# GpSimd's scaling of the softmax rows: a multiply by one column becomes a multiply by one column and an add of a column of zeros

## The chip, the cores and the metric

One core of a Trainium2 chip runs the whole program. The metric is the time of one execution on the device in microseconds; the time before is 1647.33 us, the median of 2 runs (1647.22 to 1647.44). The engines are called as the profile calls them: PE (TensorE), DVE (VectorE), ACT (ScalarE), POOL (GpSimd) and SP (SyncE, which only issues DMAs here).

## The reference

Attention over 8 batches of 8 heads, 576 positions and head size 64, with a threshold below each row's maximum, and then a feed-forward net over the 4608 tokens of 512 numbers:

```python
scores = scale * np.matmul(q, k.transpose(0, 1, 3, 2))
thresh = np.max(scores, axis=-1, keepdims=True) - tau
scores = np.where(scores >= thresh, scores, -1000000000.0)
scores = scores - np.max(scores, axis=-1, keepdims=True)
attn = np.exp(scores)
attn = attn / (np.sum(attn, axis=-1, keepdims=True) + 1e-09)
attn_out = np.matmul(attn, v)                  # 8, 8, 576, 64
x = attn_out.transpose(0, 2, 1, 3).reshape(4608, 512)
h = x @ w_in                                   # 512 to 2048
r = np.maximum(h, 0.0)
out = (s * (r * r) + b) @ w_out                # 2048 to 512
```

All is fp32.

## The kernel before, in words

The work of attention is cut into 288 tiles of 128 query rows by 576 keys. The first 36 (batch 0, "plain") use fp32 matmuls as they are. The other 252 split each operand into a high part, rounded to fp32r, and a low part, the rest, and multiply the parts; this needs more element-wise work and less of PE.

One tile i goes through the engines so. PE makes the scores into PSUM (L324). DVE copies them negated to SBUF and takes the row's minimum into a column of st (L327). ACT makes the threshold column (L331) and the exponential em (L333). DVE zeroes what lies beyond the threshold, multiplies with em and sums the rows (L336), and takes the reciprocal of the sums (L339). POOL then multiplies em, 128 x 576, in place by that column of reciprocals (L340): this is the instruction that is changed, one for each tile, 288 in all. For a split tile DVE then transposes em in blocks of 32 x 32 (L371 for 512 columns, L373 for 64), SP's queue moves the blocks with four DMAs to er (L377), ACT rounds er to eh (L387), and POOL subtracts to get the low part (L388). PE multiplies both with v (L402). For a plain tile PE transposes em (L348, L349). The tiles sm, em and tr have two buffers each, so tile i + 2 takes the buffers of tile i; the scores lie in one bank pair after the first 16 tiles.

The feed-forward net runs between: 18 blocks of 256 tokens, 16 steps each. A step is 12 matmuls (L518), Relu (L525), Square (L527) and rounding (L528) on ACT, a low part on POOL (L529 gl; for the last block on DVE) and 12 matmuls (L535). POOL has one more job, the low part of v (L276). DVE also makes the low parts of k (L272), q and qt (L292) and x (L504), and adds and takes out results (L409, L546).

The order in which each engine gets its instructions is worked out before the program is built. `Plan` is a list scheduler: each operation is added with an engine, a pair of costs in ns (how long it holds its engine, after how long its result is there), its keys read and written, and a due time in tiles; `Plan.run` lets each engine take, of what is ready by these costs, the operation due first. POOL's operations, and those marked `port`, also exclude one another in the plan. Each engine then runs its list strictly in that order, and waits on semaphores where data is not there. So a change of a cost in the plan moves instructions in the lists and changes nothing else.

Of the kernel before, what the change touches and what calls it, by code (L numbers as in the profile page):

```python
# [12 lines left out]
AF = mybir.ActivationFunctionType  # L13
ALU = mybir.AluOpType
# [88 lines left out]
def tile_attention_ffn(ctx: ExitStack, tc: tile.TileContext, qT, kT, v, tau, w_in, w_out, s, b, out):  # L103
    nc = tc.nc
    P = 128
# [22 lines left out]
    def const(name, shape, dt=F32):  # L128
        return cp.tile(shape, dt, name=name)
# [3 lines left out]
    tau_t = const("tau_t", [P, 1])  # L133
    tau0 = const("tau0", [P, 1])
    nsc = const("nsc", [P, 1])
    bias_t = const("bias_t", [P, DM])
    ones = const("ones", [P, P], F32R)
    qt = const("qt", [P, 2, P], F32R)
# [46 lines left out]
    def dve2(cost, fn, r, w, at):  # L185
        plan.add("DVE", cost, fn, r, w, at)

    def act(cost, fn, r, w, at):
        plan.add("ACT", cost, fn, r, w, at)
# [47 lines left out]
    class Head:  # L237
# [30 lines left out]
        def prepare(self, at):  # L268
            j = self.j
            khi, klo = self.kk  # L270
            act((673, 760), lambda: nc.scalar.copy(out=lazy["k"][:, 2 * j], in_=raw), self.rk, [khi], at)
            dve2((760, 830), lambda: nc.vector.tensor_tensor(  # L272
                out=lazy["k"][:, 2 * j + 1], in0=raw, in1=lazy["k"][:, 2 * j].bitcast(F32), op=ALU.subtract),
                self.rk + [khi], [klo], at)
            act((460, 540), lambda: nc.scalar.copy(out=vt[:, j, :, 0], in_=rv), self.rv, self.kv, at)
            pool((922, 950), lambda: nc.gpsimd.tensor_tensor(  # L276
                out=vt[:, j, :, 1], in0=rv, in1=vt[:, j, :, 0].bitcast(F32), op=ALU.subtract), self.rv + self.kv, self.kv, at)
            self.load_q(at)
            self.q = {}
            parts = []  # L280
            for u in self.halves:
                n = count["q"] % 2
                count["q"] += 1
                self.q[u] = (n, [f"q{n}"])
                parts.append((slice(u * NB, (u + 1) * NB), qs[n], f"q{n}", (400, 480), (500, 560)))
            if self.tail:
                self.qt = [f"qt{j}"]
                parts.insert(min(1, j), (slice(M, S), qt[:, j, j * T:(j + 1) * T], f"qt{j}", (244, 320), (300, 360)))
            for cs, dst, key, ca, cd in parts:
                act(ca, lambda dst=dst, cs=cs: nc.scalar.activation(out=dst, in_=raw[:, cs], func=AF.Copy, scale=nsc),  # L290
                    self.rq + ["nsc"], [key], at)
                dve2(cd, lambda dst=dst, cs=cs: nc.vector.scalar_tensor_tensor(  # L292
                    out=dst[D:P], in0=raw[D:P, cs], scalar=nsc[D:P], in1=dst[D:P].bitcast(F32), op0=ALU.mult,
                    op1=ALU.subtract), self.rq + [key, "nsc"], [key], at)
# [15 lines left out]
    def tile_of(ti, i):  # L310
# [8 lines left out]
        def scores():  # L319
# [8 lines left out]
            out=sb_[:, 0:S].rearrange("p (a b) -> p a b", a=2), in0=ps[:, :, 0:HS],  # L328
            scalar1=nsc if plain else 1.0, scalar2=None, op0=ALU.mult, op1=ALU.min, accum_out=st8[:, 0:1]),
            [bk, "nsc"], [sm_k, (ks_, 0)], i - SCORES_AHEAD)  # L330
        act((200, 280), lambda: nc.scalar.activation(out=st8[:, 1:2], in_=st8[:, 0:1], func=AF.Identity, bias=tau0),  # L331
            [(ks_, 0), "nsc"], [(ks_, 1)], i - 0.4)
        act((780, 870), lambda: nc.scalar.activation(  # L333
            out=ev, in_=sb_[:, 0:S], func=AF.Exp, bias=st8[:, 0:1], scale=-1.0),
            [sm_k, (ks_, 0)], [em_k], i - 0.5)
        dve2((970, 1040), lambda: nc.vector.scalar_tensor_tensor(  # L336
            out=eb, in0=sb_, scalar=st8[:, 1:2], in1=eb, op0=ALU.is_le, op1=ALU.mult,
            accum_out=st8[:, 2:3]), [sm_k, em_k, (ks_, 1)], [em_k, (ks_, 2)], i)
        dve((160, 210), lambda: nc.vector.reciprocal(out=st8[:, 4:5], in_=st8[:, 2:3]), [(ks_, 2)], [(ks_, 4)], i)  # L339
        pool((870, 900), lambda: nc.gpsimd.tensor_scalar(  # L340
            out=ev, in0=ev, scalar1=st8[:, 4:5], scalar2=None, op0=ALU.mult), [em_k, (ks_, 4)], [em_k], i)

        if plain:
            tp, tt = bank["tp"].rearrange("p (t q) -> p t q", t=NQ), bank["tt"][0:T, 0:P]
# [25 lines left out]
        def blocks():  # L370
            nc.vector.transpose(out=to[:, :, 0:NQ].rearrange("p m c q -> p m (c q)"),  # L371
                                in_=ev[:, 0:M].rearrange("p (m r) -> p m r", m=4))
            nc.vector.transpose(out=to[:, 0:2, NQ], in_=ev[:, M:S].rearrange("p (m q) -> p m q", m=2))  # L373
        dve((740, 810), blocks, [em_k], [tr_k], i + 0.5)
        t = ti.slot
        for n in range(4):
            plan.add("SP", (450, 2600), lambda n=n: nc.sync.dma_start(  # L377
# [112 lines left out]
    class Block:  # L490
# [4 lines left out]
        def stage(self, at):  # L495
            first = not count["stage"]
            count["stage"] += 1
            more = [("xh", 1), ("xl", 0), ("xl", 1)] + [(x, "t", u) for x in ("xh", "xl") for u in range(2)] if first else []
            for c in range(0, NC, 2):
                sl = slice(c, c + 2)  # L500
                kh, kl = ("xh", c // 2), ("xl", c // 2)
                act((617, 700), lambda sl=sl: nc.scalar.copy(out=xhl()[0][:, sl], in_=self.src[:, sl]),  # L502
                    self.ksrc, [kh] + (more if not c else []), at)
                dve2((710, 780), lambda sl=sl: nc.vector.tensor_tensor(  # L504
                    out=xhl()[1][:, sl], in0=self.src[:, sl], in1=xhl()[0][:, sl].bitcast(F32), op=ALU.subtract),
                    self.ksrc + [kh], [kl], at)

# [166 lines left out]
    def constants():  # L674
        make_identity(nc, ident)
        for t in qd:
            nc.gpsimd.memset(t, 0.0)
        for t in tr + [rv]:
            nc.gpsimd.memset(t, 0.0)
        for t in sm:  # L680
            nc.gpsimd.memset(t[:, S:S + 1], -3e38)
        for t in em:
            nc.gpsimd.memset(t[:, S:S + 1], 1e-9)
# [97 lines left out]
```

## Time and profile before

| | |
|---|---|
| median of the runs | 1647.33 us (1647.22 to 1647.44) |
| the profiled execution, its own time | 1645.36 us |
| its span in the profile | 1643.5 us |
| TensorE's mean granted clock | 0.943 |
| PE busy | 1376.1 us, 84% |
| POOL busy | 1240.6 us, 75% |
| DVE busy | 1119.3 us, 68% |
| ACT busy | 1016.8 us, 62% |

Busy times are sums over the span. They say how much an engine did, not whether anything waited for it: that is read from the waits and from the stretches of the span. A busy PE is not PE at its peak, because matmuls overlap and their ends are modelled. What the profile shows as POOL's spans is rough, so the start of the next instruction is the better mark of an end.

### The profile page before, as it was taken

The page shows a single profiled execution, that of the slowest core. Times are in us where ns is not written, and L with a number is a line of the kernel's source. Part 1 is how long each engine was busy: PE and PEld are TensorE (multiplying, and loading weights), DVE is VectorE, ACT ScalarE, POOL GpSimd, SP SyncE. Part 2 cuts the span into 40 slices and gives each one's busy share as a digit, 9 for nine tenths or more (in the row PEclk, how much of TensorE's full clock was granted, in tenths as well). Part 3 has the DMA queues.
Part 4 walks back from the last instruction along what each step waited for, and adds up shares of the span by engine and source line. Part 5 has one row for each costly group of instructions (what it writes and reads, how often), then busy time and mean ns, then how long its engine had stood idle before and what let it go on. Part 6 is the DMA issues. An engine that isn't in the chain of part 4 may idle for free. (4 is left out here: it accounts for less than half of the span.)

```text
span 1643.5 us, 27906 instructions
## 1 busy us (share of the span) xinstructions
PE 1376.1 (84%) x8221; PEld 1183.7 (72%) x8221; DVE 1119.3 (68%) x2533; ACT 1016.8 (62%) x2371; POOL 1240.6 (75%) x893
## 2 busy tenths in 40 slices
PE   8999878568888888778988687887888789868998
PEld 6677667457776777667876576676777688767897
DVE  6876588777878777776247777777778757756101
ACT  6777566556666667666456666666666657656543
POOL 4554499889889889988369979888988978877410
PEclk9999999669999999999999899998999989999999
DMA  9410244443444434443134434434344433443100
GB/s 317 164 35 1 60 119 107 117 103 94 111 108 106 104 95 120 103 110 78 35 76 108 109 98 98 111 95 111 98 99 108 101 95 97 115 106 98 37 14 14
DMA packets 227016, 159.04 MB, mean 97 GB/s; under 512 B 64560, under 2 KB 204848, under 8 KB 226864
## 3 DMA queue, kind: packets, MB, share of 16 engines
q1 hardware_dynamic: 226864, 157.26, 36.7%
q8 instruction: 66, 1.08, 0.3%
q14 instruction: 86, 0.70, 0.1%
HBM read 65.14 MB, written 9.44 MB: 45 GB/s over the span
## 5 line engine op out<-in xcount | busy, mean ns | idle before, releaser
L340 POOL TENSOR_SCALAR em<-em,st 128x576 f32<-128x576 f32 x288 | 557.8, 1938 | 164.4 <-DVE st L339 118.8
L388 POOL TENSOR_TENSOR er<-er,eh 128x640 fp32r<-128x640 f32 x252 | 409.5, 1627 | 55.8 <-ACT eh L387 53.4
L535 PE MATMUL o<-w,gh 128*128 128x512 f32 x1152 | 372.1, 405 | 11.3 <-DVE oo L546 9.7
L336 DVE SCALAR_TENSOR_TENSOR em<-sm,st,em 128x577 f32<-128x577 f32 x288 | 327.5, 1139 | 38.7 <-ACT em L333 18.2
L371 DVE STREAM_TRANSPOSE tr<-em 128x512 f32<-128x512 f32 x252 | 179.2, 711 | 217.2 <-POOL em L340 202.8
L529 POOL TENSOR_TENSOR gl<-g,gh 128x256 fp32r<-128x256 f32 x272 | 229.1, 848 | 112.6 <-ACT gh L528 49.1
L333 ACT ACTIVATE em<-sm,st 128x576 f32<-128x576 f32 x288 | 223.1, 775 | 141.2 <-DVE sm L327 60.4
L535 PE MATMUL o<-w,gl 128*128 128x512 f32 x576 | 239.0, 415 | 49.6 <-POOL gl L529 49.1
L518 PE MATMUL h<-xh,w 128*128 128x256 f32 x1280 | 270.8, 292 | 9.8 <-ACT g L525 5.2
L387 ACT CAST eh<-er 128x640 fp32r<-128x640 f32 x252 | 182.3, 724 | 141.4 <-DMA er<-tr 136.5
L324 PE MATMUL s<-k,q 128*128 128x288 f32 x896 | 174.1, 319 | 82.4 <-DVE sm L327 73.3
L535 PEld LDWEIGHTS o<-w,gh 128*128 128x128 f32 x1152 | 207.4, 195 | 40.5 <-DVE oo L546 10.6
L518 PEld LDWEIGHTS h<-xh,w 128*128 128x128 f32 x1280 | 219.5, 198 | 16.9 <-ACT g L525 7.5
L324 PEld LDWEIGHTS s<-k,q 128*128 128x128 f32 x896 | 142.7, 201 | 111.9 <-DVE sm L327 87.6
L327 DVE TENSOR_SCALAR_CACHE_REDUCE sm<-s 128x576 f32<-128x576 f32 x252 | 187.8, 745 | 46.9 <-PE s L324 44.9
L518 PE MATMUL tp<-xh,w 128*128 128x256 f32 x1024 | 208.7, 286 | 0.7 <-ACT g L525 0.6
L518 PE MATMUL h<-xl,w 128*128 128x256 f32 x640 | 187.9, 294 | 18.5 <-DVE xl L504 18.4
L535 PEld LDWEIGHTS o<-w,gl 128*128 128x128 f32 x576 | 111.2, 193 | 104.5 <-POOL gl L529 81.5
L518 PEld LDWEIGHTS tp<-xh,w 128*128 128x128 f32 x1024 | 171.3, 194 | 3.2 <-ACT g L525 1.1
L518 PE MATMUL tp<-xl,w 128*128 128x256 f32 x512 | 146.1, 285 | 0.0
L518 PEld LDWEIGHTS h<-xl,w 128*128 128x128 f32 x640 | 126.6, 198 | 24.2 <-DVE xl L504 22.0
L528 ACT CAST gh<-g 128x256 fp32r<-128x256 f32 x288 | 115.2, 401 | 18.3 <-PE o L535 14.1
(144 smaller groups left out, 2237.0 us busy)
## 6 DMA issues: line engine op xcount, KB each, us to landing
er<-tr SPq DMA_DIRECT2D x1008, 80.0 KB, 2.3
raw<-in_k_dram SPq DMA_DIRECT2D x128, 144.0 KB, 2.8
raw<-in_q_dram SPq DMA_DIRECT2D x96, 144.0 KB, 2.8
w<-in_moe_w_in_dram SPq DMA_DIRECT2D x16, 512.0 KB, 8.5
w<-in_moe_w_out_dram SPq DMA_DIRECT2D x16, 512.0 KB, 8.5
rv<-in_v_dram SPq DMA_DIRECT2D x64, 128.0 KB, 2.4
out_dram<-oo SPq DMA_DIRECT2D x32, 256.0 KB, 2.2
rv<-in_v_dram SPq DMA_DIRECT2D x128, 8.0 KB, 2.1
```

The lines of the kernel that those rows point to most:

```text
L324: nc.tensor.matmul(ps[:, hf, 0:HS], stat, kk[:, cs], start=(n == 0), stop=(n == len(seq) - 1))
L327: dve((840, 900), lambda: nc.vector.tensor_scalar(out=sb_[:, 0:S].rearrange("p (a b) -> p a b", a=2), in0=ps[:, :, 0:HS], scalar1=nsc if p ...
L333: act((780, 870), lambda: nc.scalar.activation(out=ev, in_=sb_[:, 0:S], func=AF.Exp, bias=st8[:, 0:1], scale=-1.0), [sm_k, (ks_, 0)], [em_ ...
L336: dve2((970, 1040), lambda: nc.vector.scalar_tensor_tensor(out=eb, in0=sb_, scalar=st8[:, 1:2], in1=eb, op0=ALU.is_le, op1=ALU.mult, accum ...
L340: pool((870, 900), lambda: nc.gpsimd.tensor_scalar(out=ev, in0=ev, scalar1=st8[:, 4:5], scalar2=None, op0=ALU.mult), [em_k, (ks_, 4)], [em ...
L371: nc.vector.transpose(out=to[:, :, 0:NQ].rearrange("p m c q -> p m (c q)"), in_=ev[:, 0:M].rearrange("p (m r) -> p m r", m=4))
L387: act((730, 820), lambda: nc.scalar.copy(out=hi(), in_=lo().bitcast(F32)), ker, [("eh", t)], i + 1)
L388: pool((1640, 1670), lambda: nc.gpsimd.tensor_tensor(out=lo(), in0=lo().bitcast(F32), in1=hi().bitcast(F32), op=ALU.subtract), [("eh", t)] ...
L518: nc.tensor.matmul(ps, w[:, c, :], x[:, c, :], start=(c == 0 and i == 0), stop=(c == NC - 1 and i == 2))
L528: act((400, 480), lambda: nc.scalar.copy(out=hi, in_=g), [f"g{k}"], [f"gh{k}"], at)
L529: do((800, 830), lambda: eng.tensor_tensor(out=lo, in0=g, in1=hi.bitcast(F32), op=ALU.subtract), [f"g{k}", f"gh{k}"], [f"gl{k}"], at)
L535: nc.tensor.matmul(bank["o"][:, t, :], a[:, ts_], w, start=(f == 0 and i == 0), stop=(f == NF - 1 and i == 2))
```

## The change

A constant tile `zero`, 128 x 1, is made and set to zero by POOL at the start. L340 gets a second operation: after the multiplication by the column of reciprocals the column `zero` is added. The values stay what they were. No DMA, no buffer of em and no other engine's operation is added or removed.

Eight pairs of costs in the plan are changed with it: those of DVE's low parts of k (760 to 950), q (500 to 680), qt (300 to 500) and x (710 to 850), of L336 (970 to 1080) and of the transposes (740 to 915), and those of ACT's threshold column (200 to 287) and of its scaling of q and qt (400 to 490, 244 to 320). The plan's cost of L340 stays at 870. The line numbers of the changed kernel are one higher from here on.

```diff
+    zero = const("zero", [P, 1])
...
-            dve2((760, 830), lambda: nc.vector.tensor_tensor(
+            dve2((950, 1020), lambda: nc.vector.tensor_tensor(
                 out=lazy["k"][:, 2 * j + 1], in0=raw, in1=lazy["k"][:, 2 * j].bitcast(F32), op=ALU.subtract),
...
-        dve2((970, 1040), lambda: nc.vector.scalar_tensor_tensor(
+        dve2((1080, 1150), lambda: nc.vector.scalar_tensor_tensor(
...
         pool((870, 900), lambda: nc.gpsimd.tensor_scalar(
-            out=ev, in0=ev, scalar1=st8[:, 4:5], scalar2=None, op0=ALU.mult), [em_k, (ks_, 4)], [em_k], i)
+            out=ev, in0=ev, scalar1=st8[:, 4:5], scalar2=zero, op0=ALU.mult, op1=ALU.add), [em_k, (ks_, 4)], [em_k], i)
...
-        dve((740, 810), blocks, [em_k], [tr_k], i + 0.5)
+        dve((915, 980), blocks, [em_k], [tr_k], i + 0.5)
...
-        for t in tr + [rv]:
+        for t in tr + [rv, zero]:
             nc.gpsimd.memset(t, 0.0)
```

The lists of all engines are longer or shorter by nothing but the one memset, and the feed-forward steps stand among the tiles much as before, but neighbours are exchanged in many places. Two of them, for the tile whose scores were the 123rd:

DVE before, in batch 2; the tile's own rows are those with em_82 and st_74, sm, em, st and tr being the tiles named above and _n the buffer:

```order
L336 SCALAR_TENSOR_TENSOR em_82,st_74<-sm_78,st_74,em_82 128x577
L292 SCALAR_TENSOR_TENSOR qt<-raw,nsc,qt 64x64
L339 RECIPROCAL st_74<-st_74 128x1
L327 TENSOR_SCALAR sm_78,st_76<-s 128x576
L336 SCALAR_TENSOR_TENSOR em_83,st_75<-sm_79,st_75,em_83 128x577
L371 STREAM_TRANSPOSE tr_80<-em_82 128x4x128
L373 STREAM_TRANSPOSE tr_80<-em_82 128x2x32
```

DVE now, the same tile; its rows are those with em_83 and st_75, since every buffer's number is one higher:

```order
L337 SCALAR_TENSOR_TENSOR em_83,st_75<-sm_79,st_75,em_83 128x577
L372 STREAM_TRANSPOSE tr_82<-em_84 128x4x128
L374 STREAM_TRANSPOSE tr_82<-em_84 128x2x32
L340 RECIPROCAL st_75<-st_75 128x1
L328 TENSOR_SCALAR sm_79,st_77<-s 128x576
L293 SCALAR_TENSOR_TENSOR qt<-raw,nsc,qt 64x64
L372 STREAM_TRANSPOSE tr_81<-em_83 128x4x128
L374 STREAM_TRANSPOSE tr_81<-em_83 128x2x32
```

Between the tile's reciprocal, which POOL's multiplication waits for, and the transposes, which wait for the multiplication, stood the next tile's L336; now the low part of qt stands there, and the transposes of the tile before have moved in front of the reciprocal.

POOL before, around the same tile's multiplication (em_82, st_74):

```order
L340 TENSOR_SCALAR em_83<-em_83,st_73 128x576
L529 TENSOR_TENSOR gl_99<-g_95,gh_97 128x256
L529 TENSOR_TENSOR gl_98<-g_94,gh_96 128x256
L388 TENSOR_TENSOR er<-er,eh 128x640
L340 TENSOR_SCALAR em_82<-em_82,st_74 128x576
L529 TENSOR_TENSOR gl_99<-g_95,gh_97 128x256
L388 TENSOR_TENSOR er<-er,eh 128x640
L340 TENSOR_SCALAR em_83<-em_83,st_75 128x576
```

POOL now (em_83, st_75):

```order
L341 TENSOR_SCALAR em_84<-em_84,st_74,zero 128x576
L530 TENSOR_TENSOR gl_99<-g_95,gh_97 128x256
L530 TENSOR_TENSOR gl_100<-g_96,gh_98 128x256
L341 TENSOR_SCALAR em_83<-em_83,st_75,zero 128x576
L389 TENSOR_TENSOR er<-er,eh 128x640
L341 TENSOR_SCALAR em_84<-em_84,st_76,zero 128x576
```

The L388 that stood between the two low parts of feed-forward steps and the tile's multiplication is gone from there, and of the two rows between this multiplication and the next one only the L389 is left.

More of the change, by code (lines that the diff above doesn't have):

```diff
@@ L284, in prepare @@
                 self.q[u] = (n, [f"q{n}"])
-                parts.append((slice(u * NB, (u + 1) * NB), qs[n], f"q{n}", (400, 480), (500, 560)))
+                parts.append((slice(u * NB, (u + 1) * NB), qs[n], f"q{n}", (490, 570), (680, 740)))
             if self.tail:
                 self.qt = [f"qt{j}"]
-                parts.insert(min(1, j), (slice(M, S), qt[:, j, j * T:(j + 1) * T], f"qt{j}", (244, 320), (300, 360)))
+                parts.insert(min(1, j), (slice(M, S), qt[:, j, j * T:(j + 1) * T], f"qt{j}", (320, 400), (500, 560)))
             for cs, dst, key, ca, cd in parts:
@@ L330, in tile_of @@
             [bk, "nsc"], [sm_k, (ks_, 0)], i - SCORES_AHEAD)
-        act((200, 280), lambda: nc.scalar.activation(out=st8[:, 1:2], in_=st8[:, 0:1], func=AF.Identity, bias=tau0),
+        act((287, 370), lambda: nc.scalar.activation(out=st8[:, 1:2], in_=st8[:, 0:1], func=AF.Identity, bias=tau0),
             [(ks_, 0), "nsc"], [(ks_, 1)], i - 0.4)
@@ L503, in stage @@
                     self.ksrc, [kh] + (more if not c else []), at)
-                dve2((710, 780), lambda sl=sl: nc.vector.tensor_tensor(
+                dve2((850, 920), lambda sl=sl: nc.vector.tensor_tensor(
                     out=xhl()[1][:, sl], in0=self.src[:, sl], in1=xhl()[0][:, sl].bitcast(F32), op=ALU.subtract),
```

## The prediction

> **What bounds the kernel now.** The page first: busy shares, and the 40 slices for the engine that the change touches.
>
> ```profile
> PE 1376.1 (84%) x8221; PEld 1183.7 (72%) x8221; DVE 1119.3 (68%) x2533; ACT 1016.8 (62%) x2371; POOL 1240.6 (75%) x893
> ...
> POOL 4554499889889889988369979888988978877410
> ```
>
> POOL's 75% is an average over a quiet start, a long middle at 9 tenths, dips, and an end without it. So I cut the span into four kinds of stretch: the plain batch (0 to 200 us), the middle where POOL is full (200 to 700 and 900 to 1300), the stretches rich in feed-forward work (700 to 900 and 1300 to 1530), and the end. Busy us of each engine, instructions in brackets:
>
> ```profile
> 0.00:200.00 200.00, 187.49 (x1126) 141.48 (x1126) 141.24 (x322) 135.70 (x326) 96.92 (x76) 0.99 0.35 116
> ...
> sum 900.00, PE 722.03 PEld 628.80 DVE 697.82 ACT 574.88 POOL 799.91; mean PE 361.02 PEld 314.40 DVE 348.91 ACT 287.44 POOL 399.96
> ...
> sum 430.00, PE 361.24 PEld 319.06 DVE 264.88 ACT 259.34 POOL 324.99; mean PE 180.62 PEld 159.53 DVE 132.44 ACT 129.67 POOL 162.50
> ...
> 1530.00:1643.00 113.00, 105.31 (x662) 94.36 (x661) 15.32 (x30) 46.92 (x116) 18.80 (x24) 0.98 0.07 19
> ```
>
> In the first stretch PE is busy for 93.7%. In the 900 us of the middle POOL is at 88.9%, PE at 80.2%, DVE at 77.5%: POOL sets the pace. In the 430 us of the third kind PE leads with 84.0%, POOL 75.6%. In the end PE works alone.
>
> Then the waits, to see whether anybody waits for POOL. First over the whole span, then DVE's for 200 to 700 and for 900 to 1300, then PE's for 700 to 900 and for 1300 to 1530 (us in total, times, longest):
>
> ```profile
> DVE tr L371 <- POOL em L340: 202.8, 199, 3.0
> POOL em L340 <- DVE st L339: 118.8, 90, 6.9
> PE s L324 <- DVE sm L327: 77.3, 60, 4.0
> PE tp L348 <- POOL em L340: 2.4, 2, 1.3
> ...
> DVE tr L371 <- POOL em L340: 68.4, 73, 2.0
> ...
> DVE tr L371 <- POOL em L340: 64.8, 66, 2.3
> ...
> PE s L324 <- DVE sm L327: 9.6, 9, 3.7
> PE o L535 <- POOL gl L529: 6.6, 7, 2.5
> PE pv L402 <- POOL er L388: 3.2, 3, 1.4
> PE tt L402 <- POOL er L388: 2.9, 3, 1.4
> ...
> PE o L535 <- POOL gl L529: 7.4, 6, 2.3
> PE tt L402 <- POOL er L388: 5.0, 6, 1.5
> PE s L324 <- DVE sm L327: 2.0, 3, 1.1
> ```
>
> DVE stands 202.8 us in front of its transposes for this very multiplication, 199 times of 252. Behind the waiting transposes on DVE's list is the L327 that empties the score banks, and PE waits 77.3 us for that. So a late L340 reaches PE by way of DVE.
>
> **What one multiplication costs now.** POOL's groups, then the fastest and median L340 (ns), and one place of the timeline that shows the duration against the next start:
>
> ```profile
> L340 POOL TENSOR_SCALAR em<-em,st 128x576 f32<-128x576 f32 x288 | 557.8, 1938 | 164.4 <-DVE st L339 118.8 <-ACT xt L366 7.9 <-PE tt L349 6.1
> L388 POOL TENSOR_TENSOR er<-er,eh 128x640 fp32r<-128x640 f32 x252 | 409.5, 1627 | 55.8 <-ACT eh L387 53.4 <-PE tp L518 1.0 <-DMA raw<-in_q_dram 0.4
> L529 POOL TENSOR_TENSOR gl<-g,gh 128x256 fp32r<-128x256 f32 x272 | 229.1, 848 | 112.6 <-ACT gh L528 49.1 <-PE o L535 42.2 <-issue 15.2
> L276 POOL TENSOR_TENSOR v<-rv,v 128x320 fp32r<-128x320 f32 x64 | 58.6, 915 | 17.2 <-ACT v L275 17.0
> L679 POOL MEMSET tr<- 128x640 f32 x2 | 1.2, 631 | 0.0
> L677 POOL MEMSET er<- 128x128 f32 x2 | 0.3, 204 | 0.0
> L681 POOL MEMSET sm<- 128x1 f32 x2 | 0.1, 98 | 0.0
> ...
> L340 POOL TENSOR_SCALAR em<-em,st x288: 1712/1730/2834, 10.4 to 1527.9; 128x576 f32<-128x576 f32 x144
> ...
> 609.50 2.23 POOL L340 TENSOR_SCALAR em<-em,st 128x576 f32<-128x576 f32 x1
> 611.70 0.73 POOL L529 TENSOR_TENSOR gl<-g,gh 128x256 fp32r<-128x256 f32 x1
> ...
> 611.76 0.71 DVE L371 STREAM_TRANSPOSE tr<-em 128x512 f32<-128x512 f32 x1 [1.62 <-POOL em L340]
> ```
>
> The next instruction starts 2.20 us after an L340 of 2.23, so the durations can be trusted here, and DVE's 1.62 us of waiting end with it. The subtractions L388 and L529, with two inputs, give a line: (1627 - 848) / (640 - 256) = 2.03 ns an element and 329 ns fixed; at 320 it says 978 where L276 has 915. At 576 elements it gives 1497. The multiplication reads one input less and yet takes 1938 on average and never under 1712, 3.0 ns an element. So neither reading nor writing sets its time, but the way in which POOL carries out this form; another form may be carried out another way. The memsets give the rate of writing alone: (631 - 204) / 512 = 0.834 ns an element, 97 fixed, 578 at 576 elements.
>
> **The change part by part.** *The new form of L340, 288 times.* No row shows a multiplication and addition on POOL. Lower bound: the memset line, 578 ns. Upper bound: as now and one more pass at the memset rate, 1938 + 480 = 2418. Between them stands the two-input line, the nearest row of arithmetic on POOL with ordinary reading and writing. I take that line less the pass for the second input, 1497 - 480 = 1017, and add the second column. A column instead of a constant costs 813 - 745 = 68 ns on DVE, the only rows with that difference:
>
> ```profile
> L327 DVE TENSOR_SCALAR_CACHE_REDUCE sm<-s 128x576 f32<-128x576 f32 x252 | 187.8, 745 | 46.9 <-PE s L324 44.9
> L327 DVE TENSOR_SCALAR_CACHE_REDUCE sm<-s,nsc 128x576 f32<-128x576 f32 x28 | 22.8, 813 | 16.8 <-PE s L324 16.6
> ```
>
> So 1017 + 68 = 1085 ns, a saving of 853 ns each. The Trainium skill, "GPSIMD Engine Reference", section 3.1, gives about 1.8 cycles an element for a good loop and no charge for a second operation where reading and writing bound it; at 1.2 GHz I estimate 576 x 1.8 / 1.2 = 864 ns from it; by that price POOL would save 40 us more in the middle, and the sum below would not move, since DVE and PE set it. The same page, section 4.1, calls operations with one input roughly line-rate on GpSimd, which would leave nothing to gain here; the trace disagrees, with 1712 ns for the fastest L340 against 578 on the memset line.
>
> *The middle, 900 us.* L340 and L336 there:
>
> ```profile
> sum 900.00, POOL 352.63; mean POOL 176.31
> ...
> L336 DVE SCALAR_TENSOR_TENSOR em<-sm,st,em 128x577 f32<-128x577 f32 x288 | 327.5, 1139 | 38.7 <-ACT em L333 18.2 <-ACT st L331 18.0 <-issue 0.4
> ...
> L336 DVE SCALAR_TENSOR_TENSOR em<-sm,st,em x288: 772/1084/2247, 8.5 to 1525.1; 128x577 f32<-128x577 f32 x144
> ```
>
> 352.63 / 1.938 = 182 multiplications; 182 x 0.853 = 155 us come off POOL, 799.9 to 645, 72% of the stretch. POOL then no longer sets the pace. Next are DVE and PE. L336 takes 1139 on average and 772 at its fastest; I put the 367 ns down to POOL being at work beside it, 182 x 0.367 = 67 us, and let it shrink with POOL's busy time, by 155 / 800 = 19%: 13 us. DVE: 697.8 - 13 = 685. If DVE as the leading engine reaches the 88.9% that POOL reaches, the stretch needs 685 / 0.889 = 770. PE, at the 93.7% of the first stretch, needs 722 / 0.937 = 771. I take 770: 130 us less. The Trainium skill, "SBUF — State Buffer", section "Who interferes with whom", says that a GpSimd instruction and a DVE instruction with two SBUF inputs exclude each other for the whole of one of them. The spread of L336 and L340 agrees. With blocking for the rest of an instruction the relief would be larger than my 13 us; the sum goes by 13, because PE's 771 would stand anyway.
>
> *The feed-forward stretches, 430 us.* PE leads. At 93.7% its 361 us would need 386, 44 less; that is all that can go. Of its 69 us idle, the rows quoted above for POOL (25.1) and for DVE's L327 (11.6) make 36.7, 53%: 0.53 x 44 = 24 us less.
>
> *The plain batch and the end.* PE waits 2.4 us for L340: 2 us less. Elsewhere the multiplication is covered by matmuls: POOL is busy for 97 of 200 us there, so even 39 longer ones would fit. In the last 113 us there is none: nothing.
>
> *The order.* The changed costs move neighbours. In the place shown the next tile's L336 (1139 ns) leaves the gap between reciprocal and transposes, L327 and the low part of qt remain, about 0.75 + 0.6 us by means (the latter by this row):
>
> ```profile
> L292 DVE SCALAR_TENSOR_TENSOR qt<-raw,nsc,qt 64x64 fp32r<-64x64 f32 x56 | 33.5, 599 | 8.5 <-ACT qt L290 7.4
> ```
>
> That covers a multiplication of 1085 ns if POOL is free then, and leaves up to 0.6 us of DVE idle a tile if it is still 1938. I cost the order at nothing with the short form, since as often something is put into the gap as is taken out; its bounds are that shortfall at a quarter of the 252 tiles either way, 63 x 0.6 = 38 us. The memset of `zero` is one column, 98 ns by the row of sm above, in front of POOL's first tile; it is left out.
>
> *The sum.* 130 + 24 + 2 = 156 us off the profiled execution's 1645.4 gives 1489; the median is 2 us higher, so 1491.
>
> **The rivals.** *The wait moves on.* POOL gets short, but DVE's transposes then wait for the next late thing (the tile buffers in pairs, ACT's exponential, the DMAs to er), and only half of the idle time returns: (68.4 + 64.8) / 2 = 67 in the middle, 12 outside instead of 26: 1647 - 79 = 1568. For it: four engines above 60% in strict order. Against it: what else DVE waits for in front of the transposes is small so far:
>
> ```profile
> L371 DVE STREAM_TRANSPOSE tr<-em 128x512 f32<-128x512 f32 x252 | 179.2, 711 | 217.2 <-POOL em L340 202.8 <-DMA er<-tr 12.0 <-DMA raw<-in_q_dram 1.4
> ```
>
> *The form is no shorter.* The added zero is carried out in the same way at the same 1.7 to 1.9 us, or drops out altogether; then only the order changes, 1647 with the 38 us either way, most likely within 20. For it: the number of elements read and written is the same. Against it: 3.0 ns an element is already above the two-input line.
>
> *The second operation is a second pass.* Then L340 takes 1938 + 480 + 68 = 2486, 548 more. In the middle POOL rises by 100 to 900, and 900 / 0.889 = 1012, 112 more; in the 430 us POOL reaches 84% and level with PE, I put 10 there: 1647 + 122 = 1769. The loss passes 2% (33 us) when the mean exceeds 1.938 + 33 x 0.889 / 182 = 2.10 us. For it: an operation is added and none removed. Against it: writes of the memsets take 0.83 ns an element, so a pass has room in 3.0.
>
> **How the numbers follow.** My forecast has 0.68, the moved wait 0.16, the unchanged form 0.08, the second pass 0.08. The forecast's own range: at 578 ns a multiplication, with PE's busy 722 shrunk by 5% as its waits inside bursts go, 686 / 0.937 = 732 in the middle, 168 less, and all 44 and 2: 1647 - 214 = 1433; on the two-input line (1565 with the column) POOL has 732 / 0.889 = 823, 77 less, and 10 elsewhere: 1560. With the order's 38 us partly on either end and the moved wait included, 1420 to 1600; it leaves out most of the last two cases. Two per cent, 33 us, is about what a measurement here tells from no change: faster by more 0.84, within 0.08, slower 0.08.
>
> **What would show it.** L340's group: a mean near 1.1 us, not 1.9. DVE's wait for POOL em at the transposes: well under 100 us instead of 202.8. POOL's slices in the middle: 7 instead of 9, with DVE and PE at 9. L336's mean under 1139. The forecast is wrong in its first step if L340's mean is above 1.6, and in its second if L340 is short and the span is still above 1600: then the waits that have grown on DVE and PE name the cause.

## The result and the profile after

The changed kernel takes 1559.49 us (median of 2 runs, 1555.59 to 1563.38), against 1647.33 before: a ratio of 0.9467, with a 95% interval of 0.9365 to 0.9569. That is 5.3% faster and inside the range of 1420 to 1600; the forecast of 1491 promised 156 us, and 88 came. The profiled execution took 1563.38 us with a span of 1561.5, 82 us less than the span before. All line numbers are one higher from here on.

First the page of the changed kernel: busy us of the engines, and how busy POOL is in 40 equal slices of the span, in tenths.

```profile
PE 1366.9 (88%) x8221; PEld 1192.2 (76%) x8221; DVE 1096.6 (70%) x2533; ACT 1011.0 (65%) x2371; POOL 992.6 (64%) x894
...
POOL 2232268667777687967438778797788676766310
```

POOL has lost 248 us of work and nearly all its nines. The groups say that this is the multiplication: L389 is as before and L530 a little longer.

```profile
L389 POOL TENSOR_TENSOR er<-er,eh 128x640 fp32r<-128x640 f32 x252 | 410.4, 1629 | 155.7 <-ACT eh L388 145.4 <-DMA er<-tr 3.3 <-PE s L325 2.5
L341 POOL TENSOR_SCALAR em<-em,st,zero 128x576 f32<-128x576 f32 x288 | 297.0, 1032 | 182.8 <-DVE st L340 112.5 <-PE pv L365 13.0 <-PE tt L350 8.1
L530 POOL TENSOR_TENSOR gl<-g,gh 128x256 fp32r<-128x256 f32 x272 | 233.9, 865 | 149.6 <-ACT gh L529 77.1 <-PE o L536 40.9 <-issue 14.5
...
L337 DVE SCALAR_TENSOR_TENSOR em<-sm,st,em 128x577 f32<-128x577 f32 x288 | 325.0, 1132 | 60.5 <-ACT st L332 37.5 <-ACT em L334 20.5 <-issue 0.3
...
L341 POOL TENSOR_SCALAR em<-em,st,zero x288: 811/830/1932, 11.7 to 1444.4; 128x576 f32<-128x576 f32 x144
```

The mean went from 1938 to 1032 ns, the median from 1730 to 830. DVE's L337, which the forecast let shrink, stayed at 1132 (1139 before).

The stretches, cut where the same kinds of work begin and end (they hold a few tiles more or less than before, so they are compared by the tile): the plain batch, the two pieces of the middle (with the multiplications in them, then the sum of all engines), the feed-forward stretches, and the end.

```profile
0.00:188.00 188.00, 183.24 (x1068) 136.64 (x1069) 119.79 (x288) 124.02 (x306) 51.87 (x71) 1.00 0.35 116
...
188.00:665.00 477.00, 109.29 (x104) 0.91 0.45 113
848.00:1236.00 388.00, 87.61 (x84) 0.93 0.45 113
...
sum 865.00, PE 727.25 PEld 645.48 DVE 703.87 ACT 588.83 POOL 666.62; mean PE 363.63 PEld 322.74 DVE 351.94 ACT 294.41 POOL 333.31
...
sum 392.00, PE 348.39 PEld 313.32 DVE 256.99 ACT 250.82 POOL 253.10; mean PE 174.20 PEld 156.66 DVE 128.50 ACT 125.41 POOL 126.55
...
1445.00:1561.00 116.00, 108.03 (x681) 96.79 (x679) 15.98 (x32) 47.31 (x117) 21.00 (x26) 0.98 0.07 20
```

In the middle 188 tiles now take 865 us, 4.60 each; before, 182 took 900, 4.95 each. POOL is at 77%, DVE at 81%, PE at 84%. No engine is as full as POOL was (88.9%).

Where did the waiting go? The waits over the whole span, of the changed kernel:

```profile
ACT eh L388 <- DMA er<-tr: 172.8, 155, 4.2
POOL er L389 <- ACT eh L388: 145.4, 122, 4.2
POOL em L341 <- DVE st L340: 112.5, 78, 8.1
PE s L325 <- DVE sm L328: 73.8, 47, 6.4
DVE tr L372 <- POOL em L341: 73.3, 104, 2.1
PE o L536 <- POOL gl L530: 16.2, 23, 2.0
```

and the two of before that answer to the first two rows:

```profile
ACT eh L387 <- DMA er<-tr: 136.5, 126, 3.5
POOL er L388 <- ACT eh L387: 53.4, 45, 4.5
```

DVE's wait for the multiplication fell from 202.8 to 73.3 us. In its place ACT waits longer for the DMAs to er, and POOL nearly three times as long for ACT. PE waits for DVE's L328 as much as before (77.3). The chain that ended last, on the page of the changed kernel, names the new members:

```profile
PE 36%; DMA 15%; SPq 13%; DVE 11%; POOL 9%; issue 9%; ACT 7%; DVEq 0%; POOLq 0%; ACTq 0%
DMA er<-tr 11%; PE o L536 11%; SPq L378 10%; PE h L519 6%; PE tp L519 5%; PE s L325 5%; PE pv L365 3%; POOL em L341 3%; POOL er L389 3%; DVE em L337 3%; PE tt L403 2%; POOL gl L530 2%; DVE tr L372 2%; DMA raw<-in_q_dram 2%; DVE sm L328 2%
```

28% of the chain is SP's queue (SPq, its time to issue) and the flight of DMAs, which the prediction's sum did not count; only its first rival names the DMAs to er. The chain on the page of before reaches back over a small part of its span (PE 6%, all else under 1%), so it can't be said how much of the 28% is new; the waits above are the comparison.

### The profile page after: what moved, and what is told of

It is laid out like the page before. It is cut to its first block, busy times and chain, and to the rows that moved or that the text cites. A ratio compares the mean times of both kernels' runs of the same rounds, so it can differ in the third digit from the quotient of the medians.

```text
span 1561.5 us, 27894 instructions
## 1 busy us (share of the span) xinstructions
PE 1366.9 (88%) x8221; PEld 1192.2 (76%) x8221; DVE 1096.6 (70%) x2533; ACT 1011.0 (65%) x2371; POOL 992.6 (64%) x894
## 4 chain that ended last, share of the span: by engine, by line
PE 36%; DMA 15%; SPq 13%; DVE 11%; POOL 9%; issue 9%; ACT 7%; DVEq 0%; POOLq 0%; ACTq 0%
DMA er<-tr 11%; PE o L536 11%; SPq L378 10%; PE h L519 6%; PE tp L519 5%; PE s L325 5%; PE pv L365 3%; POOL em L341 3%; POOL er L389 3%; DVE em L337 3%; PE tt L403 2%; POOL gl L530 2%; DVE tr L372 2%; DMA raw<-in_q_dram 2%; DVE sm L328 2%
## 5 line engine op out<-in xcount | busy, mean ns | idle before, releaser
L389 POOL TENSOR_TENSOR er<-er,eh 128x640 fp32r<-128x640 f32 x252 | 410.4, 1629 | 155.7 <-ACT eh L388 145.4
L341 POOL TENSOR_SCALAR em<-em,st,zero 128x576 f32<-128x576 f32 x288 | 297.0, 1032 | 182.8 <-DVE st L340 112.5
L337 DVE SCALAR_TENSOR_TENSOR em<-sm,st,em 128x577 f32<-128x577 f32 x288 | 325.0, 1132 | 60.5 <-ACT st L332 37.5
L530 POOL TENSOR_TENSOR gl<-g,gh 128x256 fp32r<-128x256 f32 x272 | 233.9, 865 | 149.6 <-ACT gh L529 77.1
L388 ACT CAST eh<-er 128x640 fp32r<-128x640 f32 x252 | 182.8, 726 | 176.8 <-DMA er<-tr 172.8
L536 PE MATMUL o<-w,gl 128*128 128x512 f32 x576 | 231.8, 402 | 16.5 <-POOL gl L530 16.2
L372 DVE STREAM_TRANSPOSE tr<-em 128x512 f32<-128x512 f32 x252 | 178.6, 709 | 89.1 <-POOL em L341 73.3
L328 DVE TENSOR_SCALAR_CACHE_REDUCE sm<-s 128x576 f32<-128x576 f32 x252 | 188.0, 746 | 42.5 <-PE s L325 40.4
L519 PE MATMUL tp<-xh,w 128*128 128x256 f32 x1024 | 212.1, 288 | 6.2 <-ACT g L526 6.2
L529 ACT CAST gh<-g 128x256 fp32r<-128x256 f32 x288 | 114.6, 401 | 24.5 <-PE o L536 20.9
```

The costliest lines, as they stand in the source:

```text
L328: dve((840, 900), lambda: nc.vector.tensor_scalar(out=sb_[:, 0:S].rearrange("p (a b) -> p a b", a=2), in0=ps[:, :, 0:HS], scalar1=nsc if p ...
L337: dve2((1080, 1150), lambda: nc.vector.scalar_tensor_tensor(out=eb, in0=sb_, scalar=st8[:, 1:2], in1=eb, op0=ALU.is_le, op1=ALU.mult, accu ...
L341: pool((870, 900), lambda: nc.gpsimd.tensor_scalar(out=ev, in0=ev, scalar1=st8[:, 4:5], scalar2=zero, op0=ALU.mult, op1=ALU.add), [em_k, ( ...
L388: act((730, 820), lambda: nc.scalar.copy(out=hi(), in_=lo().bitcast(F32)), ker, [("eh", t)], i + 1)
L389: pool((1640, 1670), lambda: nc.gpsimd.tensor_tensor(out=lo(), in0=lo().bitcast(F32), in1=hi().bitcast(F32), op=ALU.subtract), [("eh", t)] ...
L519: nc.tensor.matmul(ps, w[:, c, :], x[:, c, :], start=(c == 0 and i == 0), stop=(c == NC - 1 and i == 2))
```

## The experiments

Ratios are to the kernel before, measured beside each run on the same chip; 0.01 is 16.5 us. Where an experiment is a variation of the changed kernel, its ratio is held against 0.9467, and "us less" is the difference of the ratios times 1647.

### Form and order apart

Two runs undo one half of the change each. The first has the new form, but the plan's costs of before (nine pairs differ, not eight: six on DVE and three on ACT):

```diff
+    zero = const("zero", [P, 1])
-            out=ev, in0=ev, scalar1=st8[:, 4:5], scalar2=None, op0=ALU.mult), ...
+            out=ev, in0=ev, scalar1=st8[:, 4:5], scalar2=zero, op0=ALU.mult, op1=ALU.add), ...
```

> The new form of the multiplication with the plan's costs, and so the order, of before. If the shorter multiplication alone brings the gain (theory: form), about 1565 us, between 1550 and 1580, and the multiplication at 1.03 us. If the retuned order carries a good part of it (theory: order), above 1590. The DVE operation with two inputs that follows in the chain (1139 ns before) stays within 40 ns of that either way, if it is the subtractions on GpSimd that lengthen it and not the multiplication.

Measured: 1544.01 us, ratio 0.9397 (0.9365 to 0.9428), multiplication 1071 ns, L337 1118 ns. The second has the new costs and the old form:

```diff
-            out=ev, in0=ev, scalar1=st8[:, 4:5], scalar2=zero, op0=ALU.mult, op1=ALU.add), ...
+            out=ev, in0=ev, scalar1=st8[:, 4:5], scalar2=None, op0=ALU.mult), ...
```

> The retuned costs and their order with the multiplication of before, no column of zeros. Theory form: 1647 us give or take 20, the multiplication at 1.94 us. Theory order: 1620 or less. A third way is that the new order suits only a short multiplication: above 1665.

Measured: 1670.06 us, ratio 1.0187 (1.0132 to 1.0242), multiplication 1907 ns. So the form alone gives 6.0%, more than the whole change, below the window of the theory that it does it all. The retuned costs are a loss: 1.9% with the long multiplication, which is the third way that was named, and about 0.7% with the short one (0.9467 against 0.9397; the changed kernel's own interval is wide, but the next run, which differs from it by a constant, has 0.9465 with a narrow one, 0.9432 to 0.9499).

### What makes the form short

```diff
-            ... scalar2=zero, op0=ALU.mult, op1=ALU.add), ...
+            ... scalar2=0.0, op0=ALU.mult, op1=ALU.add), ...
```

> The changed kernel with the constant 0.0 as the second operand in place of the column of zeros. If two operations are what makes the form short, the multiplication takes 0.95 to 1.05 us and the time is 1559 give or take 10. If it takes two columns, it stays at 1.9 us and the time is that of the order alone, 1620 to 1665.

Measured: 1555.2 us, ratio 0.9465 (0.9432 to 0.9499). The fastest, median and slowest multiplication of this kernel:

```profile
L341 POOL TENSOR_SCALAR em<-em,st x288: 738/752/1857, 9.9 to 1433.3; 128x576 f32<-128x576 f32 x144
```

Two operations are enough. The column costs 830 - 752 = 78 ns a multiplication in the median, where the forecast took 68 from DVE, but nothing that can be measured in the kernel's time.

### Which work of GpSimd holds up DVE

In the trace before, L336 next to a subtraction and next to a multiplication. The first two rows are a pair, and so are the last two (start, duration, us):

```profile
602.16 1.56 POOL L388 TENSOR_TENSOR er<-er,eh 128x640 fp32r<-128x640 f32 x1
602.52 1.82 DVE L336 SCALAR_TENSOR_TENSOR em<-sm,st,em 128x577 f32<-128x577 f32 x1
...
604.96 1.73 POOL L340 TENSOR_SCALAR em<-em,st 128x576 f32<-128x576 f32 x1 [1.24 <-DVE st L339]
...
605.44 0.87 DVE L336 SCALAR_TENSOR_TENSOR em<-sm,st,em 128x577 f32<-128x577 f32 x1
```

The one that begins inside an L388 ends 0.62 us after it, as if it had begun to work only then; the one that begins inside an L340 takes 0.87, although the L340 has 1.25 us to go. The suspicion is that two inputs on GpSimd make the difference. Then a shorter multiplication cannot relieve L336, and a multiplication made of two inputs must hurt:

```diff
-        pool((870, 900), lambda: nc.gpsimd.tensor_scalar(
-            out=ev, in0=ev, scalar1=st8[:, 4:5], scalar2=zero, op0=ALU.mult, op1=ALU.add), ...
+        pool((870, 900), lambda: nc.gpsimd.tensor_tensor(
+            out=ev, in0=ev, in1=st8[:, 4:5].to_broadcast([P, S]), op=ALU.mult), ...
```

> The changed kernel with the multiplication as GpSimd's operation on two tensors, the column repeated along the row. By the line of the other two-input operations it takes 1.5 us. Theory: a two-input operation on GpSimd holds up DVE's two-input operations until it ends, a one-input operation hardly does; then DVE's L337 (1132 ns with the change) rises to 1250 or more although GpSimd is busy for less than before the change, and the time is 1620 to 1680. Rival: DVE's lengthening goes with GpSimd's busy time whatever the kind; then L337 stays at 1130 to 1150 and the time is 1600 to 1620.

Measured: 1598.15 us, ratio 0.9723 (0.9681 to 0.9765). Three groups of it:

```profile
L341 POOL TENSOR_TENSOR em<-em,st 128x576 f32<-128x576 f32 x288 | 377.1, 1313 | 180.8 <-DVE st L340 130.3 <-PE pv L365 8.5 <-ACT em L334 5.9
...
L337 DVE SCALAR_TENSOR_TENSOR em<-sm,st,em 128x577 f32<-128x577 f32 x288 | 337.3, 1175 | 46.7 <-ACT st L332 23.7 <-ACT em L334 20.1 <-issue 0.3
L293 DVE SCALAR_TENSOR_TENSOR q<-raw,nsc,q 64x256 fp32r<-64x256 f32 x112 | 104.4, 937 | 16.5 <-ACT q L291 14.3
```

L337 missed both windows: 1175, neither 1250 nor 1130 to 1150, and the time is close to the rival's window. The lengthening appeared elsewhere: q's low part went from 787 to 937 ns, qt's from 514 to 782, and DVE is busy for 1158 us, 61 more than with the change. Those have two inputs too, and lie beside the multiplication more often: 25 of 112 of q's and 17 of 56 of qt's begin inside it, but only 23 of the 288 L337; q's 25 take 1133 ns on average, the 24 so placed in the changed kernel 671. So this run alone doesn't settle it. The opposite one says more: the subtraction L389 replaced by an operation with one input that takes longer.

```diff
-        pool((1640, 1670), lambda: nc.gpsimd.tensor_tensor(
-            out=lo(), in0=lo().bitcast(F32), in1=hi().bitcast(F32), op=ALU.subtract), ...
+        pool((1640, 1670), lambda: nc.gpsimd.tensor_scalar(
+            out=lo(), in0=lo().bitcast(F32), scalar1=nsc, scalar2=None, op0=ALU.mult), ...
```

> The changed kernel with GpSimd's subtraction L389 (two inputs, 1629 ns) replaced by the long one-operation multiplication by a column (one input; it leaves out the low part's subtraction). GpSimd becomes busier, by some 0.3 us a tile, 75 us in all. Theory: it is the two-input kind that holds up DVE's two-input operations; L337 falls from 1132 to 900 ns or less, DVE's busy time from 1097 to 1000 or less, and the time to 1500 to 1545, although GpSimd does more. Rival: DVE is lengthened by whatever GpSimd does; L337 stays above 1100, and the time is 1560 to 1620.

```profile
PE 1349.2 (87%) x8221; PEld 1181.4 (76%) x8221; DVE 987.2 (64%) x2533; ACT 1009.1 (65%) x2371; POOL 1033.5 (67%) x894
...
L389 POOL TENSOR_SCALAR er<-er,nsc 128x640 fp32r<-128x640 f32 x252 | 489.7, 1943 | 149.2 <-ACT eh L388 140.8 <-PE tt L403 2.0 <-DMA er<-tr 1.6
...
L337 DVE SCALAR_TENSOR_TENSOR em<-sm,st,em 128x577 f32<-128x577 f32 x288 | 257.9, 898 | 75.9 <-ACT st L332 47.5 <-ACT em L334 25.8 <-issue 0.3
```

POOL does 41 us more, and yet L337 falls to 898 and DVE's busy time by 109 us to 987: it is the kind of operation, not the busy time. The second half of the expectation failed: 1551.31 us, ratio 0.9428 (0.9400 to 0.9456), 6 us less instead of 15 to 60. Taking 109 us of work from DVE buys next to nothing. That was the first sign that DVE does not set the pace either.

The number of inputs is not what makes the kind, though. Counted over whole traces, for those L336 that begin inside an operation of POOL with at least 0.4 us of it left: in the kernel before, all 124 inside a subtraction (91 in L388, 28 in L529, 5 in L276) end 0.55 to 0.70 us after it, and none of the 53 inside an L340 does. But with the constant as second operand, all 11 inside a multiplication of two operations end 0.6 us after it, and so do 7 of 10 in the changed kernel. Beside the other three the multiplication is long instead. One of each from the changed kernel (start, duration, us):

```profile
505.99 1.25 POOL L341 TENSOR_SCALAR em<-em,st,zero 128x576 f32<-128x576 f32 x1
506.73 1.11 DVE L337 SCALAR_TENSOR_TENSOR em<-sm,st,em 128x577 f32<-128x577 f32 x1
...
547.07 1.40 POOL L341 TENSOR_SCALAR em<-em,st,zero 128x576 f32<-128x576 f32 x1
547.08 0.85 DVE L337 SCALAR_TENSOR_TENSOR em<-sm,st,em 128x577 f32<-128x577 f32 x1 [1.78 <-ACT st L332]
```

So the short form, with one tensor read, takes turns with L337 as the subtractions do; the long form of one operation is the exception. The waiting goes both ways: the 80 multiplications of the changed kernel that overlap no DVE operation with two inputs take 0.81 to 0.83 us, the 208 others 1.11 on average, and that makes the mean of 1032. The Trainium skill, "SBUF — State Buffer", section "Who interferes with whom", has a DVE instruction with two SBUF inputs contend with a GpSimd instruction that reads SBUF; the trace agrees for the subtractions (124 of 124) and the short multiplication, and not for the long one (0 of 53).

### Who sets the pace now

Three more reliefs, each with the changed kernel's lists. GpSimd, the multiplication over half the columns:

```diff
-            out=ev, in0=ev, scalar1=st8[:, 4:5], scalar2=zero, ...
+            out=ev[:, 0:HS], in0=ev[:, 0:HS], scalar1=st8[:, 4:5], scalar2=zero, ...
```

> The changed kernel, with the multiplication over the first 288 of 576 columns (it leaves out the scaling of the other half); the order of all lists is the changed kernel's. It takes 0.4 us and more off GpSimd a tile, some 125 us in all. Theory: GpSimd no longer sets the pace, DVE and PE do together; the time falls by 15 us at most, to 1540 or more. Rival: GpSimd still sets it; the time falls by 60 us or more, to 1495 or less.

Measured: 1549.68 us, ratio 0.9410 (0.9390 to 0.9429), 9 us less. DVE, without the transposes of the last 64 keys:

```diff
-            nc.vector.transpose(out=to[:, 0:2, NQ], in_=ev[:, M:S].rearrange("p (m q) -> p m q", m=2))
```

> The changed kernel without the second transposes of a split tile (it leaves out the last 64 keys in the blocks), 202 ns of DVE a tile, 51 us in all. Theory: DVE and PE set the pace together, with waits between them, so that a part of the 51 comes back: 10 to 35 us, 1520 to 1547. If DVE alone sets it: 45 us or more. If PE alone, or the waits for the DMAs: under 8.

Measured: 1551.02 us, ratio 0.9422 (0.9395 to 0.9448), 7 us less. PE, without one of the six matmuls of each step's second half (1152 + 576 of L535 in 288 steps: six a step, not the twelve said in the description of the kernel):

```diff
                 for i, (a, w) in enumerate(((hi, wo[0][f]), (hi, wo[1][f]), (lo, wo[0][f]))):
+                    if t == 0 and i == 1:
+                        continue
```

> The changed kernel without one of the six products of a feed-forward step's second half (for the first 128 tokens the high part of g times the low part of w_out is left out): 2 of the 12 matmuls... of 512 columns in each pair, 288 matmuls of some 0.23 us, 66 us of PE in all, of which 8 in the end where PE works alone. Theory: the pace is shared, 20 to 45 us less, 1510 to 1540. If PE alone sets it: 60 us or more. If DVE alone, only the end's 8 and the feed-forward stretches' part: under 20.

Measured: 1549.87 us, ratio 0.9406 (0.9380 to 0.9432), 10 us less. So POOL no longer sets the pace, as the theory said. But the theory's other half, that DVE and PE do, failed: both miss their windows, with 7 and 10 us. The 7 us (under 8) are what was named for PE alone or the waits for the DMAs, the 10 us (under 20) what was named for DVE alone, which the 109 us taken off DVE above contradict. All four reliefs have intervals that overlap that of the changed kernel, so 6 to 10 us is about the noise.

The profiled executions, cut at the same tiles (the starts of the L337 of the 37th, 141st, 169th and 253rd tile), show where the little comes from. The two pieces of the middle take 864.0 us together in the changed kernel and 863.7 with the constant. They take 857.8 with POOL's lighter multiplication, 856.7 without DVE's second transposes, 862.9 without PE's matmuls (27 us of PE's work in there) and 862.8 with L389 replaced (82 us of DVE's work in there, though each L389 is 0.3 us longer, which may hide a gain). Of what PE gains, 7 us lie behind the last tile's L337, where it works alone. The time from the first to the 37th L337 varies from 173.1 to 179.5 us among these runs in no order that goes with their edits, and is noise.

That left what the chain of waits names: SP's queue. It issues four DMAs a tile to er and the loads of k, q and v. Two rows of the changed kernel: the time that one issue to er takes (ns; fastest, median, slowest), and twelve issues in a row (start, duration, us):

```profile
L378 SPq DMA_DIRECT2D er<-tr x1008: 542/602/1772, 192.7 to 1451.1; - x168
...
1030.19 8.43 SPq L378 DMA_DIRECT2D er<-tr  x12
```

One issue holds the queue for some 0.6 us (8.43 / 12 = 0.70 with the waits between), so four of them for 2.4 of a tile's 4.60 us, before any load. All issues together fill the queue for 634 of the middle's 865 us, 73% (before, 618 of 900, 69%): it isn't full, but a tile passes through it between DVE and ACT. Two runs make that queue lighter. Without the two small loads of v's last rows, and with three DMAs a tile in place of four:

```diff
-                dma(8, lambda m=m: nc.sync.dma_start(...), [], [("rv", 1 + m)], at)
+                dma(8, lambda m=m: None, [], [("rv", 1 + m)], at)
```

> The changed kernel without the two small loads of v's last 64 rows for each head of the split batches (it leaves those rows of v out; 8 KB each, 112 of the 128 or all of them in the split part), some 0.6 us of SP's queue each, 77 us of it in all, and next to no data. Theory: SP's queue, which no step of the prediction looked at, now sets the pace; DVE, PE and GpSimd wait for what it hands out. Then the time falls by 30 to 70 us, to 1485 to 1527. Rival: no single engine or queue sets it, each tile goes round a loop of waits through all of them; then as with the other reliefs 5 to 15 us, 1542 to 1552.

Measured: 1539.12 us, ratio 0.9348 (0.9321 to 0.9374), 20 us less; 128 issues are gone. The interval lies below that of the run with the constant, but just overlaps the changed kernel's wide one.

```diff
-            plan.add("SP", (450, 2600), lambda n=n: nc.sync.dma_start(
+            plan.add("SP", (450, 2600), lambda n=n: (n == 3 and i >= 52) or nc.sync.dma_start(
```

> The changed kernel with three DMAs to er in place of four for each tile from the 53rd on (it leaves out one of four blocks of 32 query rows), 236 DMAs of 0.62 us, 146 us of SP's queue; the last DMA of a tile also lands some 0.6 us earlier. Theory SP: 60 to 130 us less, 1430 to 1500. Rival loop: the tile's round gets 0.6 us shorter but the engines' lists keep each other waiting; 10 to 30 us less, 1527 to 1547.

Measured: 1509.62 us, ratio 0.9170 (0.9148 to 0.9192), 49 us less. Its chain and two of its waits:

```profile
PE 48%; POOL 12%; DVE 10%; DMA 9%; issue 8%; ACT 7%; SPq 5%; POOLq 0%; DVEq 0%; ACTq 0%
...
POOL er L389 <- ACT eh L388: 91.2, 83, 4.3
...
ACT eh L388 <- DMA er<-tr: 69.5, 84, 3.7
```

Both results lie between the two theories' windows. In time won for time taken off (for the queue the expected 77 and 146), SP's queue gives 20 / 77 = 0.26 and 49 / 146 = 0.34. The engines, by the change of their busy time, give 9 / 68 (POOL), 7 / 32 (DVE), 10 / 49 (PE) and 6 / 109 (DVE, with POOL 41 us busier). The quotients of the engines rest on differences as small as the noise, so their order is not shown. The 49 us are clear of it, and most of them come in the stretch that was forecast too short: the middle, cut as above, takes 833.4 us in place of 864.0 (856.4 without the small loads). So the way of a tile through SP's queue to er is the largest limit that was found. But it is not the only one: two thirds of what the queue gives up are waited away elsewhere. Which share belongs to the issues, which to the earlier landing of a tile's last DMA, and which to a quarter less to move, was not separated.

### A version that was to be better

The fastest version that computes the reference is the new form with the old costs (1544 us). With SP's queue in mind, the two loads of each k and q were made one, which reads the source twice (shown for k; the same for q):

```diff
-            for o in 0, D:
-                dma(144, lambda o=o: nc.sync.dma_start(out=raw[o:o + D], in_=kT[self.bi, self.h]), ...
+            dma(288, lambda: nc.sync.dma_start(out=raw, in_=kT[self.bi, self.h].unsqueeze(0).broadcast_to([2, D, S])), ...
```

> The version with the new form and the plan's old costs (1544 us), and the two loads of each k, and of each piece of q, made one load that reads the source twice, so that one issue fills both halves of the partitions; the result is the reference's. It saves about 120 issues of some 0.6 us on SP's queue, 72 us, with the same data moved. At the worth that the lighter queue had in the run without the two small loads (77 us of issue for 18 us of time), 15 to 20 us less: 1520 to 1532. If it is not the issues on SP's queue but the landing of the four DMAs to er that counts, nothing: 1538 to 1550.

Measured: 1886.38 us, ratio 1.1450 (1.1394 to 1.1506). Some of the longest pieces of its chain show why (start, us), and below it the same load as two DMAs in the changed kernel, median us from issue to landing:

```profile
596.41 8.64 DMA er<-tr
606.56 8.34 DMA raw<-in_k_dram
619.14 6.77 DMA er<-tr
...
631.49 8.39 DMA raw<-in_k_dram
```

```profile
er<-tr SPq DMA_DIRECT2D x1008, 80.0 KB, 2.2
raw<-in_k_dram SPq DMA_DIRECT2D x128, 144.0 KB, 2.7
```

One DMA of 288 KB with a repeated source takes 8.3 us where two of 144 KB took 2.7 each, and DMAs to er that meet such a load take 6.8 to 8.6 instead of 2.2. The size alone is not it: three of the four plain loads of k, 288 KB with nothing repeated, landed after 2.8 to 3.8 us in the changed kernel (the fourth, 16 us into the span, after 9.6). The saving of issues is buried under that. The granted clock of PE is lower too, 0.875 against 0.950 with two loads, and PE is busy for 1475 us against 1352, so not all of the loss is waiting for loads. The last run added a truer cost for SP in the plan:

```diff
-            plan.add("SP", (450, 2600), lambda n=n: nc.sync.dma_start(
+            plan.add("SP", (620, 2700), lambda n=n: nc.sync.dma_start(
```

> The same with one cost in the plan changed: a DMA to er holds SP's queue for 620 ns instead of 450, as the trace has it, and lands after 2700. If the loss by the retuned costs came from costs that were right but not complete (SP's was left too low), a complete plan is better: 1500 to 1520. If any other order is as good or bad as the next, it scatters by 15 us around the version without it.

Measured: 1846.3 us, ratio 1.1218 (1.1170 to 1.1265). It lies 40 us under the run before it, more than scatter by the 15 us expected, but on top of slow loads it says nothing about the plan of the changed kernel.

## Why the prediction was right, and where it was not

**The multiplication.** Taken at 1085 ns, measured 1032. That it would be short was right; that the number fits is luck. The way to it, the two-input line less a read pass, is not how the time is made up: by the half-width run, 588 ns in the median at 288 columns and 830 at 576 make 0.84 ns an element and 346 fixed, so that an element costs what it costs a memset (0.834). Undisturbed the form takes 820 ns, and its waits for DVE, which the forecast did not count, raise the mean to 1032.

**The middle.** That POOL gives up the lead was right (77% busy, forecast 72). The size was wrong: 130 us forecast, (4.95 - 4.60) x 182 = 64 measured. This is the term that was mis-sized, and in it the step that failed is "if DVE as the leading engine reaches the 88.9% that POOL reaches". The demands were right: DVE's 704 us for 188 tiles are 3.74 a tile, the forecast's 685 for 182 are 3.76; PE's are 3.87 and 3.97. The shares were not: DVE reached 81.4%, PE 84.1%. A share that one engine reached as the only full one was handed to two engines, and SP's queue was not in the list of candidates. The reliefs of DVE and PE show that neither leads: 27 us of PE's work taken off the middle leave it as long as it was, to about 1 us, and so do 82 us of DVE's, though with a longer L389. What holds the other 66 us back is shown in part only: 31 of them come back in the middle when er's DMAs are three a tile in place of four, and the retuned order takes 17 (the middle is 847.2 us with the form alone).

**The relief of L336.** 13 us for a less busy POOL: wrong mechanism. L336 stayed the same (1132), because the subtractions hold it up and not the long multiplication: 101 of 288 begin inside an L388 before, and 101 inside an L389 now. So its spread, taken as a sign that L340 blocks it, was not that. It cost the sum little, since the low parts of k, qt and x did become shorter (1047 to 963, 599 to 514, 1065 to 968 ns).

**The feed-forward stretches.** 24 us forecast. Now 65 tiles take 392 us, 6.03 each; before, 67 took 430, 6.42 each: 26 us. Right, in the time; the waits that it was taken from were not checked one by one.

**The plain batch and the end.** 2 us less and nothing were forecast; the 37th tile's L336 starts 188.9 us into the span instead of 183.4, and the end is 3 us longer. Together: 64 + 26 - 5 - 3 = 82, the difference of the spans. The 5 us are within the noise: with the constant, the way to the same place takes 6 us less than with the column.

**The order.** Costed at nothing with 38 us either way. It costs about 11 us with the short multiplication, and with the long one 31 by the ratio or 25 by the medians (1670.06 against 1645.02), a loss inside those bounds. The prediction's own reason bears this out: with L336 gone from the gap in front of the transposes, a long multiplication has less to hide behind; DVE's wait there is 221.4 us in the run with the order alone, 202.8 before.

**The rivals.** The moved wait was given 0.16 and 1568 us. Its number is the nearest, to within 9 us, and of the next late things that it names "the DMAs to er" is one that grew. But not at the place that it names, so the 9 us are partly luck too: in front of DVE's transposes the wait for er stayed at 12 us and the idle time fell from 217.2 to 89.1 us,

```profile
L372 DVE STREAM_TRANSPOSE tr<-em 128x512 f32<-128x512 f32 x252 | 178.6, 709 | 89.1 <-POOL em L341 73.3 <-DMA er<-tr 11.8 <-POOL gl L530 1.5
```

while ACT and POOL wait behind them. The unchanged form and the second pass are excluded by the row of L341 in the groups.

## What to carry to other kernels

Before a gain is booked, list the next limits with the queues that issue DMAs among them, at so many issues a tile by the time of one issue, and don't give two engines that feed each other the share of an engine that was full alone. To find who leads after such a change, lighten one resource at a time with the order of all lists held still, and compare the time won with the time taken off; here no resource returned much more than a third, and several returned no more than the noise. Costs in a planner that are closer to the trace one by one need not make a better order: retune after a change only with a run of the change alone beside it.

## What was not expected of the hardware

A GpSimd operation of one tensor by a column took 1730 ns in the median at 576 columns and 1885 at 640 (the replaced L389), 2.4 ns an element between these two; with a second operation, on a column or a constant, 830 and 752 at 576, and with the column 0.84 ns an element between 288 and 576. The Trainium skill, "GPSIMD Engine Reference", section 3.1, has bodies of up to two operations bound by the ports at 1.03 cycles an element, which I estimate as 0.86 ns at its 1.2 GHz: the form with two operations agrees, the one with a single operation takes almost three times that.

DVE's L336, with two inputs, ends 0.6 us after a GpSimd subtraction or a multiplication with two operations in which it begins; beside a multiplication with a single operation it takes little longer than at its fastest (0.97 us on average over the 53 counted inside an L340, 772 ns the fastest; 898 on average with a long L389 of that kind, 1132 with the subtraction). Why the long form does not hold it up is open.

One DMA that reads its source twice through a repeated outer dimension took 8.3 to 8.4 us in the places shown, two plain ones of half the size 2.7 each, and it held up others behind it. The Trainium skill, "DMA: Bandwidth & Descriptors", section "Rules for kernel authors", warns of this shape: a leading zero-stride copy of size c confines the whole DMA to at most c of the 16 engines. The times agree with it; on how many engines the load ran was not read from the trace.
